# Routing of the last tile and its hand-over to the experts: copies by halves, counts and scatter tags after the selection, three small groups kept side by side

## Chip, cores and metric

The kernel runs on one core of a Trainium2 chip. The metric is device microseconds of that core from launch to end, as the median of several runs; the profile shows one execution more, instruction by instruction.

## The reference

Three stages follow each other on 2304 tokens (4 sequences of 576) of 512 features.

1. Windowed attention: 8 heads of 64, each query sees itself and the 63 keys before it, with a softmax over them.
2. A wide layer: `h = x @ w_in` (512 to 2048), `g = h * tanh(softplus(h))`, `x = g @ w_out` (2048 to 512).
3. Eight experts. What the routing does, in the reference's own lines:

```python
do_compute = x @ w_skip > 0
logits = xc @ w_gate                      # xc = x[do_compute], 8 columns
e_idx = np.argmax(logits, axis=1)
gate_w = softmax(logits)[e_idx]
y[mask] = gate_w * (relu(xc[mask] @ w1[e]) @ w2[e])   # mask: e_idx == e
out[do_compute] = xc + y                  # other tokens: out = x
```

## The kernel before

The work is written as tasks of a plan: each names its engines, what it comes after, which buffers it takes and a due time. The planner puts the tasks in one order by its own costs, and the instructions are recorded in that order; each engine then runs its own list strictly in order and waits on semaphores. There are two plans. The first holds attention, the wide layer and the routing, the second the experts.

**First plan.** The tokens go through in six blocks of 384 (m = 0 to 5), each of three tiles of 128 tokens (t = 0 to 2). For each block PE forms the 16 chunks of the wide layer and sums them in three PSUM tiles `po[m, t]`. Then for each tile: `xe` copies `po` to the SBUF tile `xs` (with a minus sign), `xo` stores it to the output, `rT` transposes it on PE, `re` copies the transposed tile to `xf`, and `rl` multiplies it by the gate's columns. For the first five blocks a `Group` of three tiles follows, with one instruction for all three; for the last block (m = 5, called L) there are three groups of one tile. A group's operations, nearly all on DVE with 8 columns or 1, are: `m1`, `su`, `dm`, `fi`, `m2`, `oh` (which expert, as a one-hot row), `pl` on PE (how many tokens before this one have the same expert, from the running counts `cum` and a triangular matrix), `pi`, `ro`, `ke` (the row number, kept in `row_all`), `sl` (the slot as an integer `r_si`), `sm`, `ep`, `ga`, `tg` (the gate, written as a tag into the last columns of `xs`), and `co` (adds the one-hot rows to `cum`). Last, `sd` scatters the tile's rows, by an indirect DMA that POOL issues, to the table `xg_d` in DRAM, where each expert has 256 slots.

**Hand-over.** Expert 0 does not wait for the last block's scatter. Its table as the first five blocks left it is loaded (`bl`) and transposed into PSUM (`bt`, tile `sel`); from the last block, the rows are split into two parts `xsH`, `xsL` (`sH`, `sL`), `pm` makes a 0/1 matrix `pick` from `row_all`, and `se2` adds by four multiplications for each tile t and half i the rows that belong to expert 0. `xgH` copies the two halves of `sel` to `xgT`, the input of expert 0. In the gaps that the planner sees on PE, warm-up multiplications with 128 columns (`warm`) are recorded. Behind the first plan stands `rounds()`: nine small DVE operations that make the counters `nrounds`, `level` and `folded` from the counts; SP reads `nrounds` before its first load of the experts, PE reads `level` before the fourth group of the first expert.

**Second plan.** For each expert e: `xg` loads its 256 rows (two loads), `xT` transposes them, `E1` multiplies by w1 in four groups `fp` of two 128-column chunks, ReLU and split follow (`hH` on ACT, `hL` on DVE), `E2` multiplies by w2, `y` combines and `dl` scatters to the output. SP issues the loads of rows (`xg`) and weights (`st`, `w`); the transposition of expert e+1 stands between the E2 steps of expert e. The w2 weights of experts up to 2 that are loaded early are split (`eH`, `eL`) in the first plan.

Of the kernel before, what the change touches and what calls it, by code (L numbers as in the profile page):

```python
# [9 lines left out]
F32 = mybir.dt.float32  # L10
# [12 lines left out]
N1 = 144  # L23
# [148 lines left out]
def tile_kernel(  # L172
# [654 lines left out]
    def x_evac(eng, m, t):  # L827
# [6 lines left out]
        G.tensor_copy(xs[:, DM + 1:XW].bitcast(I32), tok[:, n:n + 1])  # L834

    def x_store(m, t):
        n = 3 * m + t
        SP.dma_start(out=out[128 * n:128 * n + 128, :], in_=xs_t[m, t][:, :DM])
# [6 lines left out]
    def route_Te(eng, m, t):  # L845
        if m == NB - 1:
            xf = rqp.tile([128, NK, 128], F32, tag="rk", name="xf", bufs=4)
        else:
            xf = sml.tile([128, NK, 128], F32, tag="xf", name="xf", bufs=1)
        copy(eng, xf, xf_t[m, t])  # L850
        xf_t[m, t] = xf

    def route_few(m, t):
# [25 lines left out]
    class Group:  # L879


        def __init__(self, m, t0, n):
            self.m, self.t0, self.n, self.i = m, t0, n, 3 * m + t0

# [40 lines left out]
        def place(self):  # L925
            self.pp = pp = ps_s.tile([128, self.n, NE], F32, tag="ps", name="pp")
            for t in range(self.n):
                PE.matmul(pp[:, t], ones8, cum, start=True, stop=False)
                for t2 in range(t):
                    PE.matmul(pp[:, t], ones8, self.oh[:, t2], start=False, stop=False)  # L930
                PE.matmul(pp[:, t], triu8, self.oh[:, t], start=False, stop=True)
# [65 lines left out]
    for m in range(NB):  # L997
# [3 lines left out]
        for t in range(3):  # L1001
            T(("xe", m, t), two(.48, .6), lambda e, m=m, t=t: x_evac(e, m, t), after=[("L2t", NF * m + NF - 1, t) if last else ("L2", NF * m + NF - 1)],
              get=[("xs", ("xs", m, t))], use=[("po", m, t)], due=tb + 2)
            T(("xo", m, t), one(SS, .45), lambda e, m=m, t=t: x_store(m, t), after=[("xe", m, t)], lat=2.5,
              due=tb + 20, use=[("xs", m, t)])
            T(("rT", m, t), one(PP, .43), lambda e, m=m, t=t: route_T(m, t), after=[("xe", m, t)] + [("re", m, t - 1)] * (t > 0),
              get=[("ps", ("rtp", m, t))], due=tb + dt * (2 + 2 * t), use=[("xs", m, t)])
            T(("re", m, t), two(.48, .6), lambda e, m=m, t=t: route_Te(e, m, t), after=[("rT", m, t)],
              get=[("rk" if last else "xf", ("xf", m, t))], use=[("rtp", m, t)])
# [6 lines left out]
            T(("rl", m, t), one(PP, .75), lambda e, m=m, t=t: route_lg(m, t), after=[("re", m, t), ("wg",)],  # L1016
              get=[("ps", ("lp", m, t))], use=[("xf", m, t)], due=tb + dt * (3 + 2 * t))
# [4 lines left out]
        prev = None  # L1022
        for t0, n in ([(t, 1) for t in range(3)] if last else [(0, 3)]):
            g = Group(m, t0, n)
            lgs = [("lg", m) if n > 1 else ("rl", m, t0)]
# [5 lines left out]
            def R(name, eng, cost, fn, after, use=(), late=0.0, get=(), lat=None, g=g, gb=gb, td=td):  # L1031
# [9 lines left out]
            R("oh", VV, .1, Group.onehot, [key("m2")])  # L1041
            R("pl", PP, .1, Group.place, [key("oh")] + ([prev("co")] if prev else [("co", m - 1, 0)] if m else []),
              get=[("ps", ("pp", m, t0))])
            R("pi", VV, .1, Group.pick, [key("pl")], [("pp", m, t0)], .5)
            R("ro", VV, .1, Group.row, [key("pi")], (), .5)
            R("sl", VV, .07, Group.slot, [key("ro")], (), .5)
            R("ke", VV, .07, Group.keep, [key("ro")], (), .3 if last else 6)
            R("sm", VV, .1, Group.sum, [key("se")], (), .5)
            R("ep", VV, .07, Group.eps, [key("sm")], (), .5)
            R("ga", VV, .09, Group.gate, [key("ep")], (), .5)  # L1050
            R("tg", VV, .07 * n, Group.tag, [key("ga")], [("xs", m, t0 + t) for t in range(n)], .5)
            R("co", VV, .21 * n, Group.count, [key("pl")], (), 1)
            for t in range(n):
# [60 lines left out]
    for t in range(3):  # L1114
        T(("sH", t), two(.52, .34), lambda e, t=t: xs_H(e, t), after=[("xe", L, t)],
          get=[("xHL", "xsHL")] if t == 0 else (), use=[("xs", L, t)], due=te + 10 + t, behind=[("sH", t - 1)] * (t > 0))
# [16 lines left out]
    for n in range(32):  # L1133
# [3 lines left out]
        if key[1] < NK:  # L1137
# [26 lines left out]
    def keep_warm(key, t0, t1):  # L1164
# [52 lines left out]
    def E1(e, fp):  # L1217
        ph_t[e, fp] = ph = pl1.tile([128, 2, N1], F32, tag="ph2", name="ph2")
        for i in range(2):
            f = 2 * fp + i  # L1220
            for kk in range(NK):
                PE.matmul(ph[:, i], w1_t[e, kk][:, 128 * f:128 * f + 128], xgT[e][:, kk, :N1],  # L1222
                          start=kk == 0, stop=kk == NK - 1)

# [241 lines left out]
```

## Time and profile before

| | us |
|---|---|
| median of 3 runs (lowest, highest) | 687.76 (687.21, 689.37) |
| the profiled execution's own time | 687.16 |
| its span, first to last instruction | 685.4 |
| PE busy in it | 670.7 (98%) |
| DVE busy | 460.1 (67%) |
| ACT busy | 405.6 (59%) |

The time is that of the whole execution; the span is what lies between its first and last profiled instruction, so 1.8 lie around it. PE counts as busy while a multiplication is anywhere in its pipeline, also when it is a warm-up or runs at the slower of its two clocks, so 98% does not say that PE is at its peak. Places in the program are given by the time from the start of the span; the first plan ends near 534.

### The profile page before, as it was taken

The numbers are of one execution on the slowest core, as the hardware profiler recorded it, in microseconds if no ns is written. First come the engines' busy times: TensorE is split into PE (matmuls) and PEld (weight loads), VectorE is DVE, ScalarE is ACT, GpSimd is POOL, SyncE is SP. The second block draws the span as 40 slices with busy tenths as digits, with TensorE's granted clock in tenths as the row PEclk, the third lists the DMA queues.
The fourth block names the chain that finished last, engine by engine and source line by source line (L and its number), as shares of the span: only waits on it lengthen the run. The fifth ranks groups of instructions, "written<-read, shape, count | busy, mean of one in ns | idle before, by whom it ended". The sixth has DMA issues, their size and how long they took to land. (4 is left out here: it accounts for less than half of the span.)

```text
span 685.4 us, 13449 instructions
## 1 busy us (share of the span) xinstructions
PE 670.7 (98%) x4870; PEld 576.7 (84%) x4870; DVE 460.1 (67%) x1298; ACT 405.6 (59%) x994; POOL 55.6 (8%) x114
## 2 busy tenths in 40 slices
PE   8999999999999999999999999999999999999995
PEld 7777767788888888888888888888889888998983
DVE  5999999876665556556776656566678574685352
ACT  5888777677667676676555565455544253543241
POOL 3000000000020001000020001000020122211111
PEclk9999999999999999999999999999999999999998
DMA  9999966776432312232311100044464677578300
GB/s 199 279 316 324 248 134 141 191 162 146 77 75 47 83 35 53 47 93 50 66 44 24 47 1 16 12 153 146 147 200 146 224 251 261 200 286 300 132 27 19
DMA packets 150493, 92.54 MB, mean 135 GB/s; under 512 B 111869, under 2 KB 128253, under 8 KB 150416
## 3 DMA queue, kind: packets, MB, share of 16 engines
q1 hardware_dynamic: 147696, 87.11, 46.5%
q0 software_dynamic: 2720, 4.42, 1.8%
q8 instruction: 46, 0.75, 0.5%
q14 instruction: 31, 0.25, 0.1%
HBM read 73.96 MB, written 17.86 MB: 134 GB/s over the span
## 5 line engine op out<-in xcount | busy, mean ns | idle before, releaser
L737 PE MATMUL ph<-xH,w 128*128 128x384 f32 x768 | 221.1, 349 | 0.1
L788 PE MATMUL po<-w,gH 128*128 128x512 f32 x480 | 154.4, 403 | 0.0
L737 PEld LDWEIGHTS ph<-xH,w 128*128 128x128 f32 x768 | 141.0, 188 | 6.1 <-issue 1.9
L737 PE MATMUL ph<-xL,w 128*128 128x384 f32 x384 | 130.1, 339 | 0.0
L745 ACT ACTIVATE u<-u 128x384 f32<-128x384 f32 x96 | 50.3, 524 | 121.5 <-DVE u L742 121.5
L788 PEld LDWEIGHTS po<-w,gH 128*128 128x128 f32 x480 | 87.3, 189 | 17.1 <-issue 1.6
L788 PE MATMUL po<-w,gL 128*128 128x512 f32 x240 | 95.0, 396 | 0.0
L764 DVE SCALAR_TENSOR_TENSOR u<-u,ph 128x384 f32<-128x384 f32 x80 | 44.1, 551 | 67.7 <-ACT u L758 67.3
L737 PEld LDWEIGHTS ph<-xL,w 128*128 128x128 f32 x384 | 72.3, 188 | 4.4 <-issue 2.6
L1222 PEld LDWEIGHTS ph<-xgT,w 128*128 128x128 f32 x512 | 63.9, 190 | 1.5 <-DVE xgT L319 0.4
L1222 PE MATMUL ph<-xgT,w 128*128 128x144 f32 x512 | 64.7, 287 | 0.4 <-DVE xgT L319 0.3
L742 DVE TENSOR_SCALAR u<-ph 128x384 f32<-128x384 f32 x96 | 53.2, 554 | 15.0 <-PE ph L737 13.8
L773 DVE TENSOR_TENSOR gL<-u,gH 128x384 fp32r<-128x384 f32 x80 | 44.5, 557 | 17.1 <-ACT gH L317 14.2
L531 ACT ACTIVATE P<-P,mx 128x128 f32<-128x128 f32 x144 | 55.8, 391 | 0.3 <-DVE mx L524 0.2
L788 PEld LDWEIGHTS po<-w,gL 128*128 128x128 f32 x240 | 45.1, 188 | 10.7
L749 ACT ACTIVATE u<-u 128x384 f32<-128x384 f32 x96 | 50.4, 525 | 2.9
L755 ACT ACTIVATE u<-u 128x384 f32<-128x384 f32 x96 | 50.2, 523 | 2.3
L758 ACT ACTIVATE u<-u 128x384 f32<-128x384 f32 x96 | 50.2, 523 | 2.3
L788 PE MATMUL po<-w,g 128*128 128x512 f32 x96 | 44.0, 594 | 0.0
L343 DVE TENSOR_TENSOR w<-st,w 128x512 fp32r<-128x512 f32 x64 | 42.6, 683 | 0.6
L1266 PE MATMUL po<-w,hH 128*128 128x512 f32 x128 | 42.6, 414 | 0.0
L1249 ACT ACTIVATE hH<-ph 128x288 fp32r<-128x288 f32 x31 | 12.7, 411 | 42.8 <-PE ph L1222 42.8
(166 smaller groups left out, 965.8 us busy)
## 6 DMA issues: line engine op xcount, KB each, us to landing
st<-in_moe_w_dram SPq DMA_DIRECT2D x64, 256.0 KB, 6.0
w<-in_moe_w_dram SPq DMA_DIRECT2D x32, 512.0 KB, 5.3
w<-in_moe_w_in_dram SPq DMA_DIRECT2D x16, 512.0 KB, 6.4
w<-in_moe_w_out_dram SPq DMA_DIRECT2D x16, 512.0 KB, 6.0
out_dram<-xs SPq DMA_DIRECT2D x18, 256.0 KB, 2.4
xg<-xg_d SPq DMA_DIRECT2D x16, 257.0 KB, 4.5
ca<-w SPq DMA_DIRECT2D x16, 256.0 KB, 3.2
xg_d<-nothing SPq DMA_DIRECT2D x16, 256.0 KB, 4.8
```

The costliest lines, as they stand in the source:

```text
L343: eng.tensor_tensor(l, raw_w.pop(key), h.bitcast(F32), op=ALU.subtract)
L531: A.activation(P[:, i], P[:, i], AF.Exp, bias=mx[:, 0, u % 2, i:i + 1], scale=-1.0, accum_out=mx[:, 1, u % 2, i:i + 1])
L737: PE.matmul(phs[c], a[:, kk], b[:, kk], start=kk == 0 and n == 0, stop=kk == NK - 1 and n == len(terms) - 1)
L742: V.tensor_scalar(u, phs[c], 20.0, None, op0=ALU.min)
L745: A.activation(us[c], us[c], AF.Exp)
L749: A.activation(us[c], us[c], AF.Square, bias=1.0)
L755: A.activation(us[c], us[c], AF.Ln, scale=0.5, bias=half_t[c])
L758: A.activation(us[c], us[c], AF.Exp, scale=-1.0)
L764: V.scalar_tensor_tensor(o, us[c], 1.0, phs[c], op0=ALU.subtract, op1=ALU.mult)
L773: eng.tensor_tensor(gL, us[c], gH.bitcast(F32), op=ALU.subtract)
L788: PE.matmul(po[m, t], a[:, ts], b, start=f == 0 and n == 0, stop=f == NF - 1 and n == len(terms) - 1)
L1222: PE.matmul(ph[:, i], w1_t[e, kk][:, 128 * f:128 * f + 128], xgT[e][:, kk, :N1], start=kk == 0, stop=kk == NK - 1)
```

## The change

The diff, without the parts that only rename or repeat:

```diff
+    def x_evac_half(eng, m, t, n):
+        if n == 0:
+            xs_t[m, t] = xsp.tile([128, XW], F32, tag="xs", name="xs")
+            G.tensor_copy(xs_t[m, t][:, DM + 1:XW].bitcast(I32), tok[:, 3 * m + t:3 * m + t + 1])
+        hs = slice(256 * n, 256 * n + 256)
+        if eng is A:
+            A.activation(xs_t[m, t][:, hs], po[m, t][:, hs], AF.Copy, scale=-1.0)
+        else:
+            V.tensor_scalar(xs_t[m, t][:, hs], po[m, t][:, hs], -1.0, None, op0=ALU.mult)
...
+    def route_Te_half(eng, m, t, n):
+        if n == 0:
+            xf_t[m, t] = (xf_t[m, t], rqp.tile([128, NK, 128], F32, tag="rk", name="xf", bufs=4))
+        p, xf = xf_t[m, t]
+        copy(eng, xf[:, 2 * n:2 * n + 2], p[:, 2 * n:2 * n + 2])
+        if n == 1:
+            xf_t[m, t] = xf
...
+        @property
+        def front(self):
+
+            return self.prev.front + [self.prev.oh[:, 0]] if self.prev else []
...
                 PE.matmul(pp[:, t], ones8, cum, start=True, stop=False)
-                for t2 in range(t):
-                    PE.matmul(pp[:, t], ones8, self.oh[:, t2], start=False, stop=False)
+                for o in self.front + [self.oh[:, t2] for t2 in range(t)]:
+                    PE.matmul(pp[:, t], ones8, o, start=False, stop=False)
...
+            if halves:
+                T(("xe", m, t), one(VV, .3), lambda e, m=m, t=t: x_evac_half(e, m, t, 0), after=done,
+                  get=[("xs", ("xs", m, t))], use=[("po", m, t)], due=tb + 2)
+                T(("xe2", m, t), one(AA, .3), lambda e, m=m, t=t: x_evac_half(e, m, t, 1), after=done,
+                  behind=[("xe", m, t)], use=[("po", m, t)], due=tb + 2)
...
-            R("pl", PP, .1, Group.place, [key("oh")] + ([prev("co")] if prev else [("co", m - 1, 0)] if m else []),
-              get=[("ps", ("pp", m, t0))])
+            R("pl", PP, .1, Group.place, [key("oh")] + ([prev("oh")] if prev else [("co", m - 1, 0)] if m else []),
+              get=[("ps", ("pp", m, t0))], use=[("grp", m, x) for x in range(t0)])
...
-            R("sl", VV, .07, Group.slot, [key("ro")], (), .5)
+            R("sl", VV, .07, Group.slot, [key("ro")] + [("pm", 2)] * last, (), .5)
...
-            R("sm", VV, .1, Group.sum, [key("se")], (), .5)
+            calm = [("pm", 2)] * last
+            R("sm", VV, .1, Group.sum, [key("se")] + calm, (), .5)
...
-            R("co", VV, .21 * n, Group.count, [key("pl")], (), 1)
+            R("co", VV, .21 * n, Group.count, [key("pl")] + calm + ([prev("co")] if prev else []) + [("pl", m, 2)] * last, (), 1)
...
-        T(("sL", t), one(VV, .6), lambda e, t=t: xs_L(e, t), after=[("sH", t)], use=[("xs", L, t)],
+        T(("sL", t), one(VV, .6), lambda e, t=t: xs_L(e, t), after=[("sH", t)] + [("xe", L, 2)] * (t == 1) + [("re", L, 2)] * (t == 2), use=[("xs", L, t)],
...
-        T(("xgH", i), two(.52, .6), lambda e, i=i: sel_H(e, i), after=[("se2", t, i) for t in range(3)],
-          get=[("xHL", "xg0")] if i == 0 else (), use=[("sel", i)], due=te + 16, behind=[("xgH", 0)] * i)
+        T(("xgH", i), one(VV if i else AA, .55), lambda e, i=i: sel_H(e, i), after=[("se2", t, i) for t in range(3)],
+          get=[("xHL", "xg0")] if i == 0 else (), use=[("sel", i)], due=te - 8, behind=[("xgH", 0)] * i)
...
-        T(("eH", key), two(.52, .34), lambda e, key=key, i=i: expert_H(e, key, i), after=[("el", key), last_use[i]],
+        T(("eH", key), two(.52, .34), lambda e, key=key, i=i: expert_H(e, key, i), after=[("el", key), last_use[i]] + [("xgH", 0), ("xgH", 1)] * (key in ((2, 5), (2, 7))),
...
-        n = int((t1 - t0 - GAP) * FILL / (0.056 if t0 else 0.085))
+        n = int((t1 - t0 - GAP) * (1.0 if stage[0] else FILL) / (0.056 if t0 else 0.085))
...
-        for i in range(2):
+        if e == 0 and fp == 0:
+            order = [(i, kk) for k2 in (0, 2) for i in range(2) for kk in (k2, k2 + 1)]
+        else:
+            order = [(i, kk) for i in range(2) for kk in range(NK)]
+        for i, kk in order:
```

In words. In the last tile of the last block (L, 2) the copy of `po` to `xs` and the copy of the transposed tile are each written as two halves of 256 columns, the first on DVE and the second on ACT. A group's place `pl` no longer waits for the counts `co` of the group before; it adds the one-hot rows of the groups before by multiplications of its own (`front`), so the three groups' buffers are held until the last `pl`. In the last block `sl`, `sm` (and with it `ep`, `ga`, `tg`) and `co` come after the last pick `pm`. The two copies of the selected rows go to ACT and DVE, one each, and are due earlier. The splits of the w2 weights 5 and 7 of expert 2 come after these copies. The first group of expert 0 takes the first two parts of the sum for both chunks before the other two. Warm-ups are counted at the full gap in the last stage, not at 0.8 of it.

What this does to the lists of the engines begins where the last block's last tile is copied. On PE the warm-ups between the first and the second place are 13 instead of 17, those ahead of the last eight selecting multiplications 4 instead of 7; the third place stands behind eight selecting multiplications instead of four, and one and two multiplications `pp<-r_oh,ones` are added to the second and third place.

DVE, from the third tile's row number to the counters, first before (names: `pp`, `r_w`, `r_r` are the steps to the row number, `gate_all` to `xs` is the tag, `w<-st` an expert 2 weight, `sel` to `xgT` the copy for expert 0, `mc`, `th` the counters):

```order
L939 TENSOR_REDUCE r_r<-r_w 128x1
L960 COPY xs<-gate_all 128x1 x2
L946 TENSOR_SCALAR row_all<-r_r 128x1
L943 TENSOR_SCALAR r_si<-r_r 128x1
L343 TENSOR_TENSOR w_6555<-st,w_6555 128x512
L1093 TENSOR_SCALAR pick<-iota_123,row_all 128x256
L319 COPY xgT<-sel 128x512 x2
L1151 TENSOR_REDUCE mc<-cp 128x1
```

and the same place in the changed program:

```order
L1132 TENSOR_SCALAR pick<-iota_123,row_all 128x256
L987 TENSOR_TENSOR cum<-cum,r_oh 128x8
L966 TENSOR_SCALAR r_si<-r_r 128x1 x2
L987 TENSOR_TENSOR cum<-cum,r_oh 128x8
L966 TENSOR_SCALAR r_si<-r_r 128x1
...
L319 COPY xgT<-sel 128x512
L976 TENSOR_SCALAR r_se<-r_se 128x1 x2
L979 RECIPROCAL gate_all<-r_se 128x1 x3
L983 COPY xs<-gate_all 128x1 x3
L319 CAST w_6732<-st 128x512
```

The tags (`xs<-gate_all`), the slots (`r_si`) and the counts (`cum`) of all three tiles stood ahead of the last pick; now the counts and slots stand between the last pick and the one copy that DVE keeps, and the tags behind that copy, followed by one cast and two subtractions for weights.

SP, at the passage to the experts, before, with what each row waits for (`DMASW` are the counts of POOL's own DMAs, the scatters among them, `DMAHW` those of SP's loads):

```order
L333 DMA st<-in_moe_w_dram 128x512 [waits DMASW4_49,DMASW3_49,DMASW5_49,DMASW2_49,DMASW7_49,DMASW1_49,DMAHW1_49,DMASW0_49,DMAHW2_49,DVE_49,DMAHW7_49,PE_49,Activation_49]
L333 DMA st<-in_moe_w_dram 128x512 [waits DMAHW0_49]
L333 DMA st<-in_moe_w_dram 128x512
L1200 DMA xg<-xg_d 128x514
L1200 DMA xg<-xg_d 128x514 [waits DMAHW3_49]
L1200 DMA xg<-xg_d 128x514 [waits DMAHW4_49]
L1200 DMA xg<-xg_d 128x514 [waits DMAHW5_49]
L1200 DMA xg<-xg_d 128x514 [waits DMAHW6_49]
```

and in the changed program:

```order
L333 DMA st<-in_moe_w_dram 128x512 [waits DMASW4_49,DMASW3_49,DMASW5_49,DMASW2_49,DMASW7_49,DMASW1_49,DMAHW1_49,DMASW0_49,DMAHW2_49,DVE_49,DMAHW7_49,PE_49,Activation_49]
L333 DMA st<-in_moe_w_dram 128x512 [waits DMAHW0_49]
L333 DMA st<-in_moe_w_dram 128x512
L1239 DMA xg<-xg_d 128x514
L1239 DMA xg<-xg_d 128x514 [waits DMAHW3_49]
L1239 DMA xg<-xg_d 128x514 [waits DMAHW4_49]
L1270 UNCONDITIONAL_BRANCH
L1239 DMA xg<-xg_d 128x514 [waits DMAHW5_49]
L1239 DMA xg<-xg_d 128x514 [waits DMAHW6_49]
L1270 UNCONDITIONAL_BRANCH
L1239 DMA xg<-xg_d 128x514 [waits DMAHW7_49]
```

The order of the loads is the same; three branch points stand elsewhere. In both, the first `st` load waits for POOL's DMAs, and the third and fourth `xg` rows are those of expert 1.

## Rows read from the trace of the kernel before

**Rows 1.** The page: busy time by engine; PE's granted clock in 40 slices, in tenths.

```profile
PE 670.7 (98%) x4870; PEld 576.7 (84%) x4870; DVE 460.1 (67%) x1298; ACT 405.6 (59%) x994; POOL 55.6 (8%) x114
...
PEclk9999999999999999999999999999999999999998
```

**Rows 2.** Stages: stretch, length, busy time (count) by engine, granted clock, DMA share, GB/s.

```profile
527.93:531.34 3.41, 3.41 (x29) 3.32 (x27) 2.74 (x31) 0.21 (x1) 0.71 (x1) 0.50 0.02 5
```

**Rows 3.** PE's waits, whole run: total us, times, longest; the second alone is in 515:560.

```profile
PE warm L1176 <- DVE ones L214: 1.1, 1, 1.1
...
PE ph L1222 <- DVE xgT L319: 0.3, 1, 0.3
```

**Rows 4.** Timeline of routing and selection: start, us, engine, line, operation, tiles.

```profile
524.35 0.68 DVE L832 TENSOR_SCALAR xs<-po 128x512 f32<-128x512 f32 x1
...
525.59 1.91 PE L873 MATMUL lp<-wgs,xf 128*128 128x9 f32 x16
...
527.57 1.71 PE L1176 MATMUL warm<-ones 128*128 128x128 bf16 x17
...
530.09 0.42 PE L1099 MATMUL sel<-pick,xsH 128*128 128x256 f32 x1
...
530.30 0.42 PE L1099 MATMUL sel<-pick,xsL 128*128 128x256 f32 x1
...
530.52 0.23 PE L928 MATMUL pp<-cum,ones 128*128 128x8 bf16 x1
...
531.35 0.68 DVE L343 TENSOR_TENSOR w<-st,w 128x512 fp32r<-128x512 f32 x1
...
531.94 0.35 DVE L1093 TENSOR_SCALAR pick<-iota,row_all 128x256 fp32r<-128x256 int16 x1
...
532.81 0.37 PE L1099 MATMUL sel<-pick,xsH 128*128 128x256 f32 x1
```

**Rows 5.** The same timeline, from the selection's end into expert 0.

```profile
533.58 1.29 DVE L319 COPY xgT<-sel 128x512 f32<-128x512 f32 x2 [1.29 <-PE sel L1099]
...
533.73 0.28 PE L1099 MATMUL sel<-pick,xsL 128*128 128x256 f32 x1
...
534.32 8.22 PE L1222 MATMUL ph<-xgT,w 128*128 128x144 f32 x64 [0.29 <-DVE xgT L319]
...
535.98 0.17 DVE L1159 SCALAR_TENSOR_TENSOR level<-cp,th 128x8 int32<-128x8 f32 x1
```

**Rows 6.** Timeline of tag and scatters, then their time to landing, then the group before.

```profile
529.73 0.14 DVE L960 COPY xs<-gate_all 128x1 f32<-128x1 f32 x1
...
530.63 0.98 POOL L279 DMA_INDIRECT xg_d<-xs,r_si  x1 [21.09 <-DVE gate_all L956]
...
533.59 0.98 POOL L279 DMA_INDIRECT xg_d<-xs,r_si  x1 [0.30 <-issue]
...
DMA to landing us min/median/max: 2.5/2.6/3.6
...
500.74 1.14 POOL L279 DMA_INDIRECT xg_d<-xs,r_si  x1 [70.27 <-DVE r_si L943]
502.18 1.48 POOL L279 DMA_INDIRECT xg_d<-xs,r_si  x1 [0.30 <-issue]
503.96 0.97 POOL L279 DMA_INDIRECT xg_d<-xs,r_si  x1 [0.31 <-issue]
```

**Rows 7.** SP: first st loads, third xg load and its landing, landing of all six.

```profile
536.95 1.37 SPq L333 DMA_DIRECT2D st<-in_moe_w_dram  x3
...
L1200 SPq DMA_DIRECT2D xg<-xg_d x1: 438/438/438, 539.3 to 539.3; - x1
...
DMA to landing us min/median/max: 4.9/4.9/4.9
...
DMA to landing us min/median/max: 4.6/5.2/6.5
```

**Rows 8.** Timeline: PE transposes expert 1's first rows.

```profile
545.64 0.61 PE L1208 MATMUL tp<-ident,xg 128*128 128x128 f32 x4
```

More of the change, by code (lines that the diff above doesn't have):

```diff
@@ L879, in tile_kernel, with __init__ @@
     class Group:
-        def __init__(self, m, t0, n):
-            self.m, self.t0, self.n, self.i = m, t0, n, 3 * m + t0
+        def __init__(self, m, t0, n, prev=None):
+            self.m, self.t0, self.n, self.i, self.prev = m, t0, n, 3 * m + t0, prev
+        @property
+        def front(self):
+            return self.prev.front + [self.prev.oh[:, 0]] if self.prev else []
         def lg(self):
@@ L1001, in tile_kernel @@
         for t in range(3):
-            T(("xe", m, t), two(.48, .6), lambda e, m=m, t=t: x_evac(e, m, t), after=[("L2t", NF * m + NF - 1, t) if last else ("L2", NF * m + NF - 1)],
-              get=[("xs", ("xs", m, t))], use=[("po", m, t)], due=tb + 2)
-            T(("xo", m, t), one(SS, .45), lambda e, m=m, t=t: x_store(m, t), after=[("xe", m, t)], lat=2.5,
+            halves = last and t == 2
+            done = [("L2t", NF * m + NF - 1, t) if last else ("L2", NF * m + NF - 1)]
+            if halves:
[4 more added lines that the diff above has]
+            else:
+                T(("xe", m, t), two(.48, .6), lambda e, m=m, t=t: x_evac(e, m, t), after=done,
+                  get=[("xs", ("xs", m, t))], use=[("po", m, t)], due=tb + 2)
@@ L1005, in tile_kernel @@
+            xe = [("xe", m, t)] + [("xe2", m, t)] * halves
+            T(("xo", m, t), one(SS, .45), lambda e, m=m, t=t: x_store(m, t), after=xe, lat=2.5,
               due=tb + 20, use=[("xs", m, t)])
-            T(("rT", m, t), one(PP, .43), lambda e, m=m, t=t: route_T(m, t), after=[("xe", m, t)] + [("re", m, t - 1)] * (t > 0),
+            T(("rT", m, t), one(PP, .43), lambda e, m=m, t=t: route_T(m, t), after=xe + [("re", m, t - 1)] * (t > 0),
               get=[("ps", ("rtp", m, t))], due=tb + dt * (2 + 2 * t), use=[("xs", m, t)])
-            T(("re", m, t), two(.48, .6), lambda e, m=m, t=t: route_Te(e, m, t), after=[("rT", m, t)],
-              get=[("rk" if last else "xf", ("xf", m, t))], use=[("rtp", m, t)])
+            if halves:
+                T(("re", m, t), one(VV, .3), lambda e, m=m, t=t: route_Te_half(e, m, t, 0), after=[("rT", m, t)],
+                  get=[("rk", ("xf", m, t))], use=[("rtp", m, t)])
+                T(("re2", m, t), one(AA, .3), lambda e, m=m, t=t: route_Te_half(e, m, t, 1), after=[("rT", m, t)],
+                  behind=[("re", m, t)], use=[("rtp", m, t)])
+            else:
+                T(("re", m, t), two(.48, .6), lambda e, m=m, t=t: route_Te(e, m, t), after=[("rT", m, t)],
+                  get=[("rk" if last else "xf", ("xf", m, t))], use=[("rtp", m, t)])
@@ L1015, in tile_kernel @@
                 continue
-            T(("rl", m, t), one(PP, .75), lambda e, m=m, t=t: route_lg(m, t), after=[("re", m, t), ("wg",)],
+            T(("rl", m, t), one(PP, .75), lambda e, m=m, t=t: route_lg(m, t), after=[("re", m, t), ("wg",)] + [("re2", m, t)] * halves,
               get=[("ps", ("lp", m, t))], use=[("xf", m, t)], due=tb + dt * (3 + 2 * t))
@@ L1021, in tile_kernel @@
             T(("lg", m), one(VV, .1), lambda e, m=m: route_lge(m), after=[("rs", m)], use=[("lp", m)])
-        prev = None
+        prev = g = None
         for t0, n in ([(t, 1) for t in range(3)] if last else [(0, 3)]):
-            g = Group(m, t0, n)
+            g = Group(m, t0, n, g)
             lgs = [("lg", m) if n > 1 else ("rl", m, t0)]
@@ L1114, in tile_kernel @@
     for t in range(3):
-        T(("sH", t), two(.52, .34), lambda e, t=t: xs_H(e, t), after=[("xe", L, t)],
+        T(("sH", t), two(.52, .34), lambda e, t=t: xs_H(e, t), after=[("xe", L, t)] + [("xe2", L, 2)] * (t == 2),
           get=[("xHL", "xsHL")] if t == 0 else (), use=[("xs", L, t)], due=te + 10 + t, behind=[("sH", t - 1)] * (t > 0))
-        T(("sL", t), one(VV, .6), lambda e, t=t: xs_L(e, t), after=[("sH", t)], use=[("xs", L, t)],
+        T(("sL", t), one(VV, .6), lambda e, t=t: xs_L(e, t), after=[("sH", t)] + [("xe", L, 2)] * (t == 1) + [("re", L, 2)] * (t == 2), use=[("xs", L, t)],
           due=te + 12 + t)
@@ L1218, in E1 @@
         ph_t[e, fp] = ph = pl1.tile([128, 2, N1], F32, tag="ph2", name="ph2")
-        for i in range(2):
+        if e == 0 and fp == 0:
+            order = [(i, kk) for k2 in (0, 2) for i in range(2) for kk in (k2, k2 + 1)]
+        else:
+            order = [(i, kk) for i in range(2) for kk in range(NK)]
+        for i, kk in order:
             f = 2 * fp + i
-            for kk in range(NK):
-                PE.matmul(ph[:, i], w1_t[e, kk][:, 128 * f:128 * f + 128], xgT[e][:, kk, :N1],
-                          start=kk == 0, stop=kk == NK - 1)
+            PE.matmul(ph[:, i], w1_t[e, kk][:, 128 * f:128 * f + 128], xgT[e][:, kk, :N1],
+                      start=(i, kk) == order[0], stop=(i, kk) == order[-1])
     def E1_second(e, fq):
```

## The prediction

> **What bounds the kernel now.** I read the page first, then the granted clock by stage, the list of PE's waits, the timeline across the change from one phase to the other, and last the POOL and SP queues. PE is busy for 98% of the span and its clock is at 9 tenths or more in every slice but the last [rows 1], so time is won or lost only where PE does little of use. Such a place is the stretch from 524.1 to 534.3, where routing of the last tile, its selection and the copy for expert 0 hang on each other; the change edits this stretch. In it PE passes for busy, but on warm-up and narrow multiplications, and its clock is 0.50 for 3.41 us [rows 2]. Between 515 and 560 PE's only listed wait is one of 0.3 us, and in the whole run none is over 1.1 [rows 3]: the expert phase is a closed row of PE work, and any moment by which its start comes earlier, or by which it stalls later, shows in the end.
>
> The chain there, as the timeline has it [rows 4]: the third tile is copied at 524.35, its logits are multiplied until 527.5, then 17 warm-ups run into the half clock. The third tile's place multiplication starts at 530.52. A subtraction of 0.68 on DVE, begun at 531.35 when the row number is ready, then stands ahead of the last pick, which starts at 531.94, and seven warm-ups let the last eight selecting multiplications start only at 532.81. They end at 534.01; two copies follow each other on DVE to 534.87, and expert 0 starts at 534.32 [rows 5].
>
> A second chain is hidden now. The first tile's gate is written to its row at 529.73, POOL starts the three scatters at 530.63 to 533.59, and the last lands 2.5 us after its start, at 536.1 [rows 6]. SP issues its first load of the expert phase at 536.95, and expert 1's first rows, the third of six xg loads, at 539.3; they land 4.9 us later, at 544.2 [rows 7]. PE takes them up at 545.64 [rows 8]. So this chain has 1.4 us to spare, and no more.
>
> **The change, part by part.** *Halves.* The third tile's copy passes a subtraction on DVE, of the size of the 0.68 of L343 [rows 4], but until 0.1 before it is transposed PE is busy with the first tile's logits anyway, and in the built program ACT's half waits on DVE's count, so the two halves don't run side by side. Bounds 0 and 0.68; I take 0.1.
>
> *Selection.* The DVE subtraction ahead of the last pick (0.68, of which 0.6 is queue time) leaves, as do two ACT copies and the small operations for counts, sums and slots. Warm-ups between the place multiplications fall from 17 to 13 and, ahead of the last eight, from 7 to 4. Against this the third place multiplication stands behind eight selecting multiplications, not four, which at the half clock's 0.21 each is 0.85 later, and three count multiplications come in at below 0.1 each. On the same clock I get the last pick some 0.2 earlier and the last eight at 532.3 instead of 532.81: 0.5 us, the 0.1 above included. The bounds are 0.2 (the half clock covers all of it) and 1.9 (it stays away: the eight selecting multiplications and the 13 warm-ups that would run in it take half). I take 0.5, since 527.5 comes in the same way as before. The selection then ends at 533.5.
>
> *Two engines for the last copy, E1 by halves.* The second copy no longer waits for the first, and the first four products of expert 0 need the first half alone: about 0.15 of the 0.3 that PE waits [rows 3]. Bounds 0 and 0.3.
>
> So PE would reach expert 1's rows at 545.64 - 0.65 = 545.0.
>
> *What is put behind the selection.* The slots' and gates' operations now come after the last pick, the tags even after the copy of the selected rows, as the DVE rows of the change show. The copy begins at 533.55 and takes 0.65, half of the 1.29 [rows 5]; then come two additions, three reciprocals and the first tag, six operations of at most 0.14 each, as the tag's own row has it [rows 6], that overlap where they don't need each other's result. Of these 0.84 I take 0.45: the first tag is written at 534.65. Scatters cannot start before: POOL took 0.75 from the tag's end (529.87) to the first scatter [rows 6], so 535.4. The third scatter followed 2.96 after the first; in the tile group before 3.22 [rows 6]. I take 3.0: 538.4, landed (2.5) at 540.9 instead of 536.1. SP's next load waits for the scatters' counts in both programs, as its rows show, and behind it in SP's queue stand three st loads and all xg loads. I give SP 0.3 after the landing (bounds 0, and the 0.8 from level at 536.14 to 536.95 [rows 5, 7], which holds the read of a counter that here is done earlier): 541.2. From SP's first load to the landing of expert 1's first rows it was 544.2 - 536.95 = 7.3, with the same transfers in the same order: 548.5. That is 4.3 later than now, of which the spare 1.4 covers a part. **PE, there at 545.0, waits 3.5 us**, and behind its waiting transposition stand the second product of expert 0 and all of expert 1. Net of the gain that is 2.85 us. Nothing behind can take it back, as PE has no idle time there. Bounds: rows that land 4.6 after their issue, the least of the six, and nothing on SP leave 2.9 of stall; a scatter that lands after 3.6, starts 3.2 apart and 0.8 on SP make it 5.3.
>
> *Clock behind the stall.* PE waits nowhere so long in this trace [rows 3], so the price is bounded: below by nothing, above by half of the 3.41 us at 0.50 [rows 2], 1.7. The clock fell after a stretch in which PE ran 9-column multiplications and short transposes; 3.5 us of nothing is emptier. I take a fall, partly under the stall itself, at 1.2. The Trainium skill (TensorE: Matmul & The Clock Gate, What's actually happening) says that the slow clock is the default and activity lifts it; by that rule too it would fall, the sum with it is 691.2 and without it 690.0, and the trace agrees for the one fall that it shows.
>
> *Edits at nothing.* The two expert-2 weight splits moved behind the copies (one cast and two subtractions of 0.68 on DVE) delay expert 0's first hL to about 536.6 and the counters to 538; expert 0's first product takes 8.2 in four groups [rows 5], of which the third needs that hL, at 537.7, and the fourth a counter, at 539.6, so 1 us of cover. If it were gone, each us would be a us.
>
> **Sum.** -0.5 - 0.15 + 3.5 + 1.2 = +4.05. Against the profiled execution's 687.16 that is 691.2; the median of the runs is 0.6 above that execution, well inside the spread of 2.2 between the runs.
>
> **Rivals.** *Stall, clock kept:* all of the above without the 1.2: 690.0. For it: PE is back at dense work at once. *No stall (the other side):* SP's loads come by 545.0. It decides where the chain from the tag is shorter by 3.5 us than I sum; only if SP's first load did not wait for the scatters, and expert 1's rows were loaded without queueing behind the three st loads, would that be so. Against it: the scatter must land in any case before rows are read, and 540.9 + 4.6 is past 545.0. Then the gain alone is left: 686.5. *Full clock in the selection:* the place multiplications come earlier, and the half clock lies elsewhere; the selection gains 1.9, but the second chain counts from its end, so the stall stays: 688.6, or 689.8 with the fall. *Scatters held by DVE:* beside the cast and the two subtractions (534.7 to 536.4) POOL could not write its lists and would start after them, at 536.4: 1.0 more, 692.2. Against it, in the group at 500.74 two scatters ran beside such work and took 1.14 and 1.48 instead of 0.98 [rows 6]. The Trainium skill (SBUF — State Buffer, Who interferes with whom) has DVE's two-port modes shut GpSimd out for the whole instruction; these rows show a part of that only.
>
> **Chances.** Stall with fall 0.50, stall without 0.25, no stall 0.12, full clock in the selection 0.08, scatters held 0.05. The forecast is the first, 691.2, its own range 689.6 to 693.0. The range over all leaves out most of "no stall" and the far ends: 688.3 to 693.0. 0.3%, 2.1 us, is about what a measurement of this kernel can tell from no change; slower by more (above 689.2) are nearly all of the first, four fifths of the second, the last and half of the fourth: 0.77. Within: 0.19. Faster, where no stall and a full clock meet: 0.04.
>
> **What would show it.** In the profile after: the last selecting multiplication ends near 533.5; expert 0's first product starts 0.25 us behind it; the first scatter starts after the copy of the selected rows, the last lands near 541; SP's first st load stands behind that; PE has one idle stretch of about 3.5 us, put down to the xg load, ahead of expert 1's transposition; the granted clock is 0.50 near it. The prediction is wrong if PE shows no idle time there, if the loads go out before the scatters land, or if the selection ends before 532.5.

## The result, and the profile after

The changed kernel takes 692.97 us (median of 5 runs, 692.27 to 693.98), the kernel before in the same comparison 687.52 (687.13 to 689.37): a ratio of 1.0072, interval 1.0053 to 1.0092. In a second comparison (run e5 below) it was 1.0085 (1.0062 to 1.0108). It is slower by 5.4 to 5.8 us; the forecast was 691.2, the range 688.3 to 693.0. The profiled execution took 692.61, with a span of 690.9 against 685.4.

The page shows little of that: PE is busy for 97% of the span, against 98% before, and one slice of its clock in the expert phase shows 8 tenths (its lines answer to [rows 1]):

```profile
PE 672.6 (97%) x4865; PEld 577.2 (84%) x4865; DVE 460.7 (67%) x1299; ACT 405.7 (59%) x995; POOL 59.0 (9%) x114
...
PEclk9999999999999999999999999999999899999998
```

The list of PE's waits does (from 500 on: us in total, times, longest; in the whole run no other wait is over 1.3). It answers to [rows 3]:

```profile
PE tp L1247 <- DMA xg<-xg_d: 3.7, 1, 3.7
PE ph L1264 <- DVE hL L1297: 0.6, 2, 0.4
```

There is one long wait, at the transposition of expert 1's rows. Its chain stands in the timeline of the selection's end and the scatters, which answers to [rows 4 to 6] (start, us, engine, line, operation, tiles):

```profile
530.99 0.35 DVE L1132 TENSOR_SCALAR pick<-iota,row_all 128x256 fp32r<-128x256 int16 x1
...
531.33 0.21 DVE L966 TENSOR_SCALAR r_si<-r_r 128x1 int32<-128x1 f32 x2
...
532.37 0.28 PE L1138 MATMUL sel<-pick,xsL 128*128 128x256 f32 x1
...
532.69 0.69 DVE L319 COPY xgT<-sel 128x512 f32<-128x512 f32 x1 [0.62 <-PE cp L1188]
...
532.87 5.41 PE L1264 MATMUL ph<-xgT,w 128*128 128x144 f32 x42 [0.20 <-ACT xgT L317]
...
533.62 0.27 DVE L983 COPY xs<-gate_all 128x1 f32<-128x1 f32 x3
533.80 0.42 DVE L319 CAST w<-st 128x512 fp32r<-128x512 f32 x1
534.13 1.29 DVE L343 TENSOR_TENSOR w<-st,w 128x512 fp32r<-128x512 f32 x2
534.51 1.17 POOL L279 DMA_INDIRECT xg_d<-xs,r_si  x1 [25.03 <-DVE w L319]
...
537.26 0.98 POOL L279 DMA_INDIRECT xg_d<-xs,r_si  x1 [0.30 <-issue]
```

The selection ends at 532.65, 1.4 earlier than before, and expert 0 starts at 532.87 instead of 534.32. The tags are written at 533.62 to 533.89 instead of 529.73 to 531.30, and the three scatters start 3.9 to 3.7 later. SP's waits between 530 and 545, its queue, and PE at expert 1's rows and at expert 1's first product answer to [rows 7, 8]:

```profile
SPq L1474 <- DVE level L1198: 11.5, 1, 11.5
SPq L333 <- DMA xg_d<-xs,r_si: 2.2, 1, 2.2
```

```profile
540.01 1.30 SPq L333 DMA_DIRECT2D st<-in_moe_w_dram  x3
541.35 3.53 SPq L1239 DMA_DIRECT2D xg<-xg_d  x6
```

```profile
547.89 1.11 PE L1247 MATMUL tp<-ident,xg 128*128 128x128 f32 x4 [3.67 <-DMA xg<-xg_d]
...
554.33 0.90 PE L1264 MATMUL ph<-xgT,w 128*128 128x144 f32 x6
```

SP first waits for the counters that DVE writes, as before; `nrounds`, which it reads, is written at 536.60. Then it waits 2.2 more for the scatters, and that wait ends last: its first load goes out 3.06 later than before, at 540.01. In the kernel before, the scatters had landed at 536.1, and it was the counter that let SP go: written at 535.66, first load at 536.95. Last, the stages around the wait (stretch, length, busy time of PE, PEld, DVE, ACT, POOL with counts, granted clock, DMA share, GB/s); the first row answers to [rows 2]:

```profile
527.93:531.34 3.41, 3.33 (x43) 3.08 (x40) 2.72 (x22) 0.21 (x1) 0.00 (x0) 1.00 0.02 5
...
544.20:547.90 3.70, 0.03 (x2) 0.01 (x1) 3.00 (x7) 0.54 (x1) 0.00 (x0) 0.80 0.93 337
547.90:553.28 5.38, 5.38 (x17) 4.50 (x18) 0.61 (x1) 2.45 (x5) 0.00 (x0) 0.50 0.99 369
553.28:562.00 8.72, 8.72 (x68) 8.50 (x68) 7.24 (x12) 4.40 (x9) 1.95 (x2) 1.00 0.50 156
```

Two things differ from before. The half clock (0.50, 1.2 GHz, the lower of its two levels) has left the selection, and it has come back behind the wait: for 5.38 us PE worked at 0.50, which by estimate costs half of that, 2.7. The kernel before has two rows for the same places:

```profile
517.27 0.49 PE L1073 MATMUL sel<-ident,base 128*128 128x128 f32 x3
...
549.54 0.65 PE L1222 MATMUL ph<-xgT,w 128*128 128x144 f32 x4
```

The first of them is the first transposition for the selection, after changed 517.64; I count from it below, since executions differ by up to 2.4 us in what lies ahead of it. So the span's 5.54 splits into +0.37 ahead of that point, -1.82 from there to expert 0 (17.05 to 15.23), +6.24 from expert 0's first product to expert 1's (15.22 to 21.46: 3.67 of wait, what is left of it, 2.57, goes to the clock), and 0.75 behind. Of these 0.67 lie in expert 5, which takes 19.18 from its first product to that of expert 6, before 18.51; 0.4 of them are a wait for `hL`.

### The profile page after: what moved, and what is told of

It reads as the page before. It is cut to its first block, busy times and chain, and to the rows that moved or that the text cites. A ratio compares the mean times of both kernels' runs of the same rounds, so it can differ in the third digit from the quotient of the medians.

```text
span 690.9 us, 13439 instructions
## 1 busy us (share of the span) xinstructions
PE 672.6 (97%) x4865; PEld 577.2 (84%) x4865; DVE 460.7 (67%) x1299; ACT 405.7 (59%) x995; POOL 59.0 (9%) x114
## 3 DMA queue, kind: packets, MB, share of 16 engines
q0 software_dynamic: 2720, 4.42, 1.7%
## 5 line engine op out<-in xcount | busy, mean ns | idle before, releaser
L1308 PE MATMUL po<-w,hH 128*128 128x512 f32 x128 | 44.0, 426 | 0.0
L279 POOL DMA_INDIRECT xg_d<-xs,r_si x18 | 19.2, 1065 | 238.7 <-DVE gH L319 74.3
```

Source lines behind the costliest of these rows:

```text
L1308: PE.matmul(po2[e, s], a[:, f, ss], b, start=f == 0 and n == 0, stop=f == 7 and n == 2)
```

## The experiments

The theory: late slots and tags make the scatters late, these hold SP's first load, so expert 1's rows come late and PE's wait brings the clock down. The rivals: the cost lies in the other edits, above all in the weight splits that now stand ahead of the round counter; or the rows are late because they queue behind three `st` loads.

The twelve profiled executions together (e5 is the changed kernel once more). "First" is the start of the first transposition for the selection; the next columns count from it to expert 0's first product, to the transposition of expert 1's rows, and to the first products of experts 1 and 2. "Wait rows" is PE's wait for expert 1's rows, "wait hL" its waits for `hL` from expert 0 on. The ratio is that of the timed runs to the kernel before on the same chip.

| kernel | first | expert 0 | rows 1 | expert 1 | expert 2 | wait rows | wait hL | ratio (interval) |
|---|---|---|---|---|---|---|---|---|
| before | 517.27 | 17.05 | 28.37 | 32.27 | 47.43 | 0 | 0.2 | 1 |
| changed | 517.64 | 15.23 | 30.25 | 36.69 | 51.74 | 3.7 | 0.6 | 1.0072 (1.0053, 1.0092) |
| e1 | 518.04 | 15.22 | 27.64 | 31.57 | 47.61 | 1.0 | 1.9 | 1.0030 (1.0012, 1.0049) |
| e2 | 517.67 | 16.61 | 29.71 | 33.64 | 48.93 | 1.7 | 1.2 | 1.0020 (1.0006, 1.0034) |
| e3 | 518.44 | 16.10 | 28.97 | 32.90 | 48.18 | 1.5 | 0.2 | 1.0014 (1.0004, 1.0025) |
| e4 | 517.73 | 16.68 | 29.12 | 33.05 | 48.78 | 0.9 | 2.3 | 1.0004 (0.9990, 1.0018) |
| e5 | 518.00 | 15.21 | 30.34 | 36.89 | 51.94 | 3.8 | 0.5 | 1.0085 (1.0062, 1.0108) |
| e6 | 518.94 | 15.23 | 29.97 | 33.90 | 49.11 | filled | 0.4 | 1.0041 (1.0024, 1.0057) |
| e7 | 518.10 | 16.42 | 28.98 | 35.13 | 51.52 | 1.2 | 1.0 | 1.0047 (1.0029, 1.0065) |
| e8 | 517.88 | 15.22 | 26.43 | 30.73 | 47.12 | 0 | 1.7 | 1.0007 (0.9990, 1.0025) |
| e9 | 519.71 | 15.22 | 27.75 | 31.68 | 47.82 | 1.2 | 0.8 | 1.0007 (0.9996, 1.0018) |
| e10 | 518.17 | 15.22 | 26.42 | 30.32 | 46.50 | 0 | 0.9 | 0.9999 (0.9981, 1.0016) |

**e1: slots and gate sums freed.**

```diff
-            R("sl", VV, .07, Group.slot, [key("ro")] + [("pm", 2)] * last, (), .5)
+            R("sl", VV, .07, Group.slot, [key("ro")], (), .5)
...
-            R("sm", VV, .1, Group.sum, [key("se")] + calm, (), .5)
+            R("sm", VV, .1, Group.sum, [key("se")], (), .5)
```

> The changed kernel with one part undone: slots and gate sums no longer wait for the last pick, everything else stays (halves, counts behind, split copies, weight splits behind the copies, own place sums). Theory (late tags and slots make the scatters late, these hold SP's first load, this makes expert 1's rows late): the scatters start near 531 and land by 537, SP's first st load goes out near 537, expert 1's rows land near 544.5, PE waits 0 to 0.5 us there, the clock stays up in the expert phase, and the time is 686.3 (685.5 to 687.5), a little under before. Rival (the gain is lost by other edits: halves, split copies, or the weight splits that stand ahead of the round counter on DVE): the time stays at 690 or above.

690.01 against 688.65. The scatters start where the theory put them (531.31), the clock stays up in the profiled execution, and 3 to 4 us of the loss are gone (1.0030 where the changed kernel has 1.0072 and 1.0085). But the rest isn't what I expected: it is not faster than before. PE's waits:

```profile
PE ph L1264 <- DVE hL L1297: 1.9, 3, 1.2
PE tp L1247 <- DMA xg<-xg_d: 1.0, 1, 1.0
```

The round counter is written at 537.07 in this execution, behind two casts and two subtractions, and SP's first load goes at 538.36, 1.3 after it, as in the kernel before (1.29). So here the rival has a part: what I had costed at nothing, the splits, holds the loads as soon as the scatters don't. The longest wait for `hL`, 1.2, is not at the hand-over but in expert 5. And this execution, 689.52, stands for eight of the twelve timed runs (688.4 to 690.3); the other four took 692.4 to 694.0 at a mean granted clock of 0.989 to 0.991 (the eight: 0.990 to 0.997). The clock may have fallen in these four as in the changed kernel; no kept trace shows it.

**e2: only gate sums and tags freed** (the second pair of e1's lines alone).

> The changed kernel with only the gate sums and tags freed; the slots still come after the last pick. Theory: the scatters start once the slots are written, near 531.7, some 2.8 us earlier than in the changed kernel, and land near 537; SP's first load goes then or at the round counter, about 537.2; PE's wait at expert 1 shrinks from 3.7 to about 0.5 to 1.2, and the time is 687.5 (686.5 to 689). Rival (it is not the scatters' start but the rest of the change): above 690, the wait at expert 1 still over 3.

690.14. The theory's time and wait were both missed, and the time is that of the rival, whose wait of over 3 is not there. The clock was 0.50 from 527.96 for 3.41 us in this execution, the last pick came at 532.44, the slots at 532.79, and the first scatter at 533.69 instead of near 531.7. SP's list has no wait for the scatters here, only one of 12.9 for the counters: `nrounds` is written at 538.02, behind the splits, and the first load goes at 539.31, 1.29 later. So it is the counter that lets SP go, as in e1. The clock stayed up behind the wait of 1.7.

**e3: only the weight splits freed.**

```diff
-        T(("eH", key), ... after=[("el", key), last_use[i]] + [("xgH", 0), ("xgH", 1)] * (key in ((2, 5), (2, 7))),
+        T(("eH", key), ... after=[("el", key), last_use[i]],
```

> The changed kernel with only the splits of the weights 5 and 7 of expert 2 freed from the copies of the selected rows, so that the round counter comes some 1.9 us earlier on DVE. Theory (the scatters hold SP): SP still waits for the landing near 539.5, PE still waits 3 to 4 us at expert 1, the time stays within 1 us of the changed kernel, 692 to 693.5. Rival (SP's first load waits for the round counter behind the weight splits): the loads go out 1.9 earlier, the wait is about 1.8 and the time 689.5 to 691.

689.79, the time that the rival gave, but not by its way. The counter is at 535.72, and SP still waits for the scatters, the last of which starts at 536.56. Counted from the first transposition that is 1.5 earlier than in the changed kernel (18.12 against 19.62), since the tags (533.09) now stand ahead of the copy, and expert 0 starts 0.9 later (16.10), since the splits are back in the selection. The rows come 1.28 earlier (28.97 against 30.25), PE 0.87 later, and its wait is 1.5 instead of 3.7; behind that the clock doesn't fall. So this kernel loses half of the gain in the selection and is some 4 us faster than the changed one. Of the 2.2 by which the wait is shorter, the lost gain makes 0.87 and the earlier rows the rest; whether the lost gain alone would have kept the clock up, no run shows.

**e4: the kernel before, with slots and gate sums behind the last pick.**

```diff
-            R("sl", VV, .07, Group.slot, [key("ro")], (), .5)
+            R("sl", VV, .07, Group.slot, [key("ro")] + [("pm", 2)] * last, (), .5)
...
-            R("sm", VV, .1, Group.sum, [key("se")], (), .5)
+            R("sm", VV, .1, Group.sum, [key("se")] + [("pm", 2)] * last, (), .5)
```

> The kernel before with one part of the change alone: slots and gate sums of the last block come after the last pick. Theory: the first tag is written near 533.3 instead of 529.7, the scatters start near 534.2 and the last lands near 539.7, SP's first load follows, expert 1's rows land near 547 and PE, ready at 545.6, waits 1 to 2 us; the time is 689.5 (688.5 to 691.5, the upper part if the clock falls behind the wait). Rival (these operations are hidden, and the cost lies in the other edits): 687.5 as before, without a wait at expert 1.

688.99 against 688.65: no difference that can be told, less than I expected. The wait is there, but only 0.9 long, since PE comes to the rows late (16.68 to expert 0) and the tags (532.87) don't stand behind a copy. The profiled execution, 691.22, is one of the slowest of the twelve: its 2.3 of `hL` include one wait of 1.8 in expert 3, which the other profiles don't have. So this part alone is harmless, and the change without it (e1) costs 0.3%: together they cost 0.7 to 0.85%. The two don't add: in the profiles each alone leaves the wait at 1.0 or less, while together PE comes to the rows some 1.7 earlier than in e4 and the rows 1.1 later, and behind that wait the clock falls.

**e5: the changed kernel again**, on the chip of the next three.

> The changed kernel itself, beside the next three and on their chip, since the four kernels above stood beside the kernel before alone. Theory: 1.005 to 1.009 of before, PE waits 3 to 4 us for expert 1's rows and the clock falls behind the wait. Rival (the profiled execution was an unlucky one): under 1.004, the wait under 2.

693.70 against 687.94, a wait of 3.8, and the clock at 0.50 behind it: the profile after was no accident.

**e6: the wait filled.** The 60 multiplications add work that nothing uses.

```diff
         tp_2[e, s] = tp = pt2.tile([128, NK, 128], F32, tag="tp", name="tp2")
+        if e == 1 and s == 0:
+            for _ in range(60):
+                PE.matmul(tp[:, 0], ones8, ones8, start=True, stop=True)
```

> The changed kernel with 60 multiplications of ones, 128 columns each, put on PE ahead of expert 1's first transposition, into the tile that it then writes. They fill about 3.4 us of the wait at full clock and compute nothing that is used. Theory (the fall of the clock is the wait's own price, about 2.5 us): the rows land as late as before, expert 1's first transposition starts near 547.9 as in the changed kernel, the granted clock stays 1.00, and the time is 2.5 lower than the changed kernel's on the same chip (2.0 to 3.0). Rival (the fall comes from elsewhere, or costs nothing): within 0.7 of the changed kernel.

691.10, that is 2.6 under e5. The timeline and the stages of e6, and then the stages of e5 for the same stretches:

```profile
545.38 3.51 PE L1248 MATMUL tp<-ones 128*128 128x128 bf16 x60
548.91 0.66 PE L1250 MATMUL tp<-ident,xg 128*128 128x128 f32 x4
```

```profile
545.00:548.40 3.40, 3.40 (x61) 3.23 (x60) 3.05 (x8) 0.55 (x1) 0.00 (x0) 1.00 1.01 346
548.40:554.00 5.60, 5.58 (x40) 4.81 (x38) 2.00 (x3) 3.68 (x7) 0.00 (x0) 1.00 1.03 385
```

```profile
545.00:548.40 3.40, 0.07 (x1) 0.07 (x2) 3.05 (x6) 0.16 (x1) 0.00 (x0) 0.82 0.94 320
548.40:554.00 5.60, 5.60 (x18) 4.62 (x19) 0.00 (x0) 2.73 (x5) 0.00 (x0) 0.50 1.02 379
```

The rows come nearly as late as in e5 (29.97 against 30.34 from the first transposition). Nine of e6's 40 multiplications in the second stretch are still the fill, so PE does 31 of its own where it did 18. From the transposition to expert 1's first product it takes 3.93 (548.91 to 552.84), in e5 6.55 (548.34 to 554.89), before 3.90: the fall costs 2.62 in these profiles, which is the 2.6 between the medians. So the fall is the wait's own second price, and the rival of a fall from elsewhere is out.

**e7: row loads ahead of the three st loads** (in the changed kernel).

```diff
-X0 = 2.6
+X0 = 0.0
```

> The changed kernel with one constant of the second plan changed, so that SP issues the six loads of rows before the three st loads. Theory (the rows wait in SP's queue behind three st loads, some 1.4 us): first row load near 540, the third near 541, expert 1's rows land near 546.4, PE waits 2.2 instead of 3.7; the time is 1.4 lower than the changed kernel if the clock falls all the same, 3.9 lower if a wait of 2.2 leaves it up (it stayed up behind waits of 1.0 to 1.7). Rival (the landing is bound by the queues and not by the issue): rows land at 547.5 or later, the time within 0.7 of the changed kernel.

692.06, 1.6 under e5. The clock does stay up, which should have given 3.9; but another wait takes its place:

```profile
PE ph L1264 <- ACT xgT L317: 2.2, 2, 2.0
PE tp L1247 <- DMA xg<-xg_d: 1.2, 1, 1.2
PE ph L1264 <- DVE hL L1297: 1.0, 2, 0.8
```

DVE's order shows why:

```profile
550.35 0.43 DVE L319 CAST w<-st 128x512 fp32r<-128x512 f32 x1 [4.89 <-DMA st<-in_moe_w_dram]
551.07 0.43 DVE L319 CAST w<-st 128x512 fp32r<-128x512 f32 x1 [0.28 <-DMA st<-in_moe_w_dram]
551.41 0.62 DVE L1297 SCALAR_TENSOR_TENSOR hL<-ph2b,hH 128x448 fp32r<-128x448 f32 x1
```

and ACT's, in the same stretch:

```profile
552.06 0.63 ACT L1321 ACTIVATE hP<-hL 128x512 fp32r<-128x512 f32 x1 [3.12 <-DVE hL L1297]
552.60 0.58 ACT L317 ACTIVATE xgT<-tp 128x512 f32<-128x512 f32 x1
```

The weights, now issued from 545.72, are there at 550.3, DVE's first cast waits 4.9 for them, and an `hL` stands behind two casts; what PE needs of ACT waits for that `hL`. (This execution had the half clock in its selection, so its scatters start 1.2 later than in e5, counted from the first transposition.) That the three st loads stood ahead of the rows was so, but changing it gains 1.6 and not 3.9, since both are needed.

**e8: slots and gate sums freed, rows first** (e1 and e7 together).

> The changed kernel with slots and gate sums freed and the row loads ahead of the st loads, which keeps the gain of the selection (expert 0 starts some 1.8 us earlier, counted from the first transposition for the selection) and should leave no wait at expert 1, since its rows land near 544. Theory: 1 to 2 us under before on the same chip, no wait for rows over 0.3. Rival (PE is then held by something next in line, the st weights or the round counter): a wait of over 0.5 in expert 0 or 1, time not under before.

688.62 against 687.94. No wait for rows is left, and expert 1 starts 1.5 earlier than before (30.73 against 32.27). At expert 2 0.3 of it are left (47.12 against 47.43): the rival's case, 0.8 of wait for `hL` in expert 1, and 0.7 in expert 5. One thing more differs here that neither edit names: SP reads the round counter only at 546.8, behind these loads, where in e1 and e7 it reads it ahead of its first load. So the first row load went out at 536.44, before the counter was written (536.83).

**e9 and e10: the round counter ahead of the weight splits**, with e1's edit, and in e10 rows first as well.

```diff
-        T(("eH", key), ... after=[("el", key), last_use[i]] + [("xgH", 0), ("xgH", 1)] * (key in ((2, 5), (2, 7))),
+        T(("eH", key), ... after=[("el", key), last_use[i]] + [("rd",)] * (key in ((2, 5), (2, 7))),
...
+    T(("rd",), one(VV, .9), lambda e: rounds_a(), after=[("co", L, 2), ("xgH", 0), ("xgH", 1)], get=[("ps", ("cp",))], use=[("cp",)], due=te - 7)
```

`rounds_a` holds the operations of `rounds()` up to `nrounds`; the others stay where they were.

> The changed kernel with slots and gate sums freed, and the five operations that make the round counter put ahead of the two weight splits; st loads stand first in SP's queue again. Theory (in e1 the scatters were no longer late, but SP's first load stood behind the round counter, 1 us later than before, and so were rows and weights): the counter is written 1.4 us earlier than in e1, SP's first load goes out at the third scatter's landing, some 0.5 to 1 us earlier than in e1, PE's wait for rows falls from 1.0 to under 0.4, the wait for expert 1's first hL (0.6 in e1) disappears, and the time is 0.5 to 1.5 under before on the same chip. Rival (weights and DVE are the next bound however early the loads are): waits for hL of over 0.5 stay in experts 0 to 2, time as before or above.

> As the run beside it, but with the six row loads ahead of the three st loads. Theory: no wait for rows at all, and st loads about 0.7 us earlier than in e8, so that the hL waits of e8 (0.8 and 0.7) shrink; 0.5 to 1.5 under before. Rival: st loads behind the rows come too late all the same, hL waits of over 0.5 at expert 1, time within 0.2% of before.

e9 takes 688.98, e10 687.67, against 688.36. Neither is faster than before, and both rivals came true: `hL` waits of 0.7 stay at expert 1. e9's profiled execution waits 1.2 for rows: its third scatter started at 535.55, and SP's first load only went at 539.15. SP's list gives 0.8 to the scatters and 0.9 to `level`, which DVE writes only at 539.02: the operations up to `nrounds` had moved ahead of the splits, that of `level` had not. In e10 SP's first load goes at 536.64, expert 1 starts 1.95 earlier than before, and at expert 2 0.93 of it are left. It is the best of the versions, and its interval holds 1. What stands against it are the loads. The stages of the kernel before and of e10 between 540 and 556:

```profile
540.00:544.00 4.00, 4.00 (x32) 3.55 (x30) 0.92 (x2) 0.82 (x2) 0.00 (x0) 1.00 0.90 303
544.00:548.00 4.00, 4.00 (x28) 3.24 (x26) 2.93 (x6) 2.63 (x5) 0.00 (x0) 1.00 1.03 377
548.00:552.00 4.00, 4.00 (x29) 3.70 (x29) 3.90 (x7) 3.31 (x6) 0.56 (x1) 1.00 0.85 288
552.00:556.00 4.00, 4.00 (x34) 3.87 (x33) 3.96 (x8) 1.89 (x5) 3.16 (x2) 1.00 0.65 258
```

```profile
540.00:544.00 4.00, 4.00 (x28) 3.38 (x27) 1.21 (x3) 0.96 (x2) 0.00 (x0) 1.00 1.01 342
544.00:548.00 4.00, 4.00 (x26) 3.23 (x25) 2.64 (x6) 2.51 (x5) 0.00 (x0) 1.00 1.05 397
548.00:552.00 4.00, 4.00 (x32) 3.88 (x31) 3.90 (x7) 3.93 (x8) 0.59 (x1) 1.00 0.98 340
552.00:556.00 4.00, 3.27 (x25) 2.89 (x24) 3.96 (x8) 0.92 (x3) 2.53 (x2) 1.00 0.37 146
```

In both, the DMA engines are at 0.85 to 1.05 from 540 to 552, and DVE is busy from 548 to 556 with hardly a gap; in e10 PE, which is ahead by then, has gaps from 552 on (busy for 3.27 of 4), in the kernel before none (4.00). The weights of expert 1 pass through both. A PE that starts earlier meets them there; this is argued from the rows, since no run made the weights themselves earlier.

## Why the prediction held, point by point

- *The half clock in the selection.* It was taken to stay, with a gain of 0.65 for halves, order and the two engines. In e7, whose first plan is the changed kernel's and which had the half clock, expert 0 starts at 16.42 against 17.05: 0.63. In the profiled execution of after, and in e1, e5, e6 and e8 to e10, the clock was 1.00 there, and the gain is 1.8, as the rival "full clock in the selection" had it (1.9, at a chance of 0.08). So the profiled selection ended at 532.65 and not at 533.5, just above the 532.5 that was named as a sign of being wrong. Which of the two an execution gets changes with the same first plan (e5 and e7). Both values are shown, in single executions.
- *The late needs.* Tags behind the copy, scatters behind them, SP's first load behind the scatters: each in the order that was forecast, and each about 1.0 earlier than the forecast's times (first scatter 534.51, forecast 535.4; first load 540.01, forecast 541.2), since the selection ended at 532.65 instead of 533.5. From SP's first load to the rows it then took 7.88 instead of 7.3. The wait counts from the same end, so it is 3.7 against 3.5. e5 repeats the chain. In e3 and e4 the scatters end SP's last wait too (2.2 and 1.6); in e1 and e2 the counter does, so earlier scatters bring the rows forward only as far as the counter lets them.
- *The clock behind the wait.* This is the term that was mis-sized: 1.2, with an upper bound of 1.7, where e6 measured 2.6. The bound was taken from the one slow stretch of the trace before in which PE works, 3.41 us; nothing in that trace made it a bound (from 681 to 685.3, with PE out of work, the clock fell a second time), and the one behind the wait lasts 6.83, of which PE works in 5.38. The kind was right and the likeliest of the rivals, "clock kept", is out. The Trainium skill (TensorE: Matmul & The Clock Gate, What's actually happening) was cited for it; the trace agrees that the clock fell after PE had been idle.
- *Edits at nothing.* The 1 us of cover that I named was reckoned for PE, which did not wait there. What the weight splits can hold is SP, which reads the counter behind them: in e1 they do. In the changed kernel the scatters' lateness covered them (SP's wait of 2.2 comes after the counter), so there the counter costs nothing.
- *Scatters held by DVE.* They were not: the first ran from 534.51 beside the two subtractions (534.13 to 535.42) and took 1.17 instead of 0.98. The rule of the Trainium skill (SBUF — State Buffer, Who interferes with whom) that was cited is one of DVE's two-port modes; the same section gives `tensor_tensor`, which these subtractions are, no such mode, so these rows don't test it.
- *The sum.* -0.65 + 3.5 + 1.2 = +4.05 was forecast; -1.82 + 3.67 + 2.57 is +4.42, and 0.37 ahead and 0.75 behind of this one execution make 5.5 of span. So the late rows, the wait and the fall came true as the likeliest case had them, but with the selection of the rival "full clock in the selection", which with the fall stood at 689.8. That the sum is so near is luck in part: the gain came out 1.17 larger and the clock's price 1.37 larger, and the two nearly cancel. The median of 692.97 lies at the very end of the range (693.0).

What stays open: why the clock stays at 1.00 in the selection of some executions (eight of the twelve, e1, e3 and e5 to e10, have another stretch of 3.41 us at 0.50 far ahead of it, between 10 and 40 us, and e7 has both), and what sets the `hL` waits of up to 1.8 in experts 3 to 5, which come and go between executions.

## What to carry to other kernels

When work is moved behind a critical stretch, follow it to the DMA that it feeds and to the queue behind that DMA: here the small operations for slots and tags, of some 0.15 us each, put behind the last pick and a copy, end in a wait of 3.7 us two transfers later. A long wait of PE has to be priced twice, once for the wait and once for the clock behind it, and the second price has no bound from slow stretches of another origin. And a gain ahead of a wait that does not move is worth nothing. It may even cost, when the longer wait is what brings the clock down; e3, faster than the changed kernel with half its gain, fits that but had its rows earlier too, so it is not shown.

## What the runs showed of the hardware

- Waits of PE of 0.9 to 1.7 us (e1 to e4, e9), and of 1.2 and 2.0 one after the other (e7), left the granted clock at 1.00 (2.4 GHz); those of 3.7 and 3.8 (changed kernel, e5) brought it to 0.50 (1.2 GHz) for 6.83 us, twice as long as the stretch in the selection, though PE was busy all the time from the wait's end on (5.38 of 5.38 us).
- Filling the wait with 60 useless multiplications of ones gave back 2.6 us of the 5.8 (e6 against e5), and the granted clock stayed at 1.00.
- From the write of the round counter to SP's first load behind it, SP's read included, it took 1.29 (before), 1.30 (e1) and 1.29 us (e2). From the start of the last scatter to its landing it took 2.5 us (before and changed kernel).
- Behind SP's first load the DMA engines are nearly always busy (share 0.85 to 1.05 from 540 to 552, before and in e10). With the rows ahead of the weights the rows came earlier (28.98 instead of 30.34 from the first transposition) and the weights were issued later (545.72 instead of 540.33), for a gain of 1.6 us (e7 against e5).
